# Attention and SwiGLU on one core: the next pair's q and k casts in three successive blocks, X loads behind the folds, four conversion steps earlier, one add on ScalarE

## The chip, the core and the metric

The kernel runs on one core of a Trainium2 chip. The metric is device time in microseconds from the start of the program to its end; three runs of the kernel before gave a median of 690.63 us (690.6 to 691.76). Engines are named as in the profile: PE is TensorE's matmul and PEld its weight load, DVE VectorE, ACT ScalarE, POOL GpSimd, and SP the engine that issues most DMAs from one queue.

## The reference

The program computes multi-head attention with rotary embeddings, and puts its output through a gated feed-forward layer. q, k and v are float32, the weights come in 64 bits, and the result is float32.

```
B, H, S, D = 4, 8, 576, 64          # attention
q, k  = rotate(q), rotate(k)
s     = (q @ k.T) / sqrt(D)
e     = exp(s - max(s))
attn  = e / (sum(e) + 1e-9) @ v
x     = attn as [2304, 512]
g     = x @ w_gate                  # [512, 1536]
y     = (g * sigmoid(g)) * (x @ w_val) @ w_out
```

## The kernel before, in words

**Two phases.** From about 11 to 277 us the kernel does attention; then, to 688 us, the feed-forward layer in products that TensorE runs almost without a gap. The 32 heads are taken as 16 pairs p. A pair has 9 blocks b of scores, and n = 9p + b numbers the blocks of the kernel. Loops run over n; in each block the named steps of PLAN["order"] (L31) are called, and tables in PLAN (L29 to L47) say in which block each step has something to do.

**One pair.** TensorE keeps float32 exact enough by splitting operands into a high and a low part. Scores of a block are four matmuls of 288 columns (L349), from QK, N and QZ, which hold the folded q and k; the ninth block takes six. ScalarE makes E with exp (L382), straight from the score's PSUM buffer sc, of which there are two. VectorE finds the maximum ahead of that (L364). TensorE transposes E through three PSUM buffers tr (L425; tails, the 64 columns left over, L435 and L437). ScalarE casts the transposed block to a high part (ET1h, ET2h, L426; TK1h, TK2h for tails, L440), and VectorE subtracts it for the low part (ET1l, ET2l, L427). The products with V (L465) use one PSUM buffer pv; ScalarE copies the result into Y (L470), and SP stores it (L484, L489, L490).

**The next pair.** Two pairs ahead, GpSimd rotates q and k into rot (L206 to L208) from X, which load_qk loads (L175). One pair ahead, the step qk_T has TensorE transpose the rotated q, k or their tail (L289, L293), and ScalarE and VectorE write high and low parts into N (cast L308, subtraction L312). After the third of these, qk_stack issues eight DMAs on SP, the folds (L319 to L326), that write QK, QZ and BD for the next pair's scores. PLAN["qk"] says in which block each of the three is done, and PLAN["qkw"] which one (2 is the tail, 0 is q, 1 is k). V is loaded as VR (L186) and split on GpSimd (L278, L279).

**Beside it.** During attention the first half of w_gate and w_val is converted from 64-bit to split float32: ten steps each (bits10), placed by PLAN["cv"], whose first entry is the block of the load (L772) and each further entry the block of one step. In pair 15 the second half begins, with its loads at L772 (f = 1) and steps on VectorE (L751 to L757). Attention's output comes back from memory as Xab (L637), is scaled by the reciprocal row sums R (L630) and split on GpSimd (L644 to L647). rsum (L389) adds 1e-9 to the row sums of four pairs and takes the reciprocal; rstore (L396) transposes and stores it.

**What sets the order.** GpSimd's instructions run in program order throughout attention, SP's until n = 48 (pair 5, block 3) and TensorE's until n = 9. All else in attention is put in an order by a scheduler, so that what the tables move also changes the order of instructions that no table names. `keep_in_program_order` takes one instruction out of that freedom. In the second phase all orders are written out by hand.

Of the kernel before, what the change touches and what calls it, by code (L numbers as in the profile page):

```python
# [14 lines left out]
ALU = mybir.AluOpType  # L15
# [13 lines left out]
    trb=3,  # L29
    warm=[9, 0, 1, 2, 0, 1],  # L30
    order=["qk", "scores", "trans", "pv", "exp", "evac", "rstore", "rope", "tails", "conv", "x", "conv1", "vsplit"],  # L31
    qk=[[3, 4, 6], [1, 2, 3], [0, 0, 1]],
    qkw=[[0, 2, 1], [2, 0, 1], [2, 0, 1]],
    tails=[4, 0],
    pv=[1, 6, 5, 3, 7, 8, 2, 7, 3],
    pv0=[0, 0, 0, 0, 0, 0, 10, 10, 2],
    lqk=0,
    lv=4,
    rope=1,
    vsplit=8,  # L40
    rstore=0,
    cv=[[13, 21, 25, 26, 28, 30, 34, 34, 44, 44, 45], [20, 30, 35, 36, 39, 41, 43, 43, 54, 54, 63]],
    xs=[[3, 3], [3, 6], [6, 5], [7, 5], [8, 7], [9, 5], [10, 5], [11, 5], [12, 7], [13, 7], [14, 1], [14, 2],
        [14, 8], [15, 0], [15, 2], [15, 4]],
    xe=[[5, 3], [6, 3], [7, 3], [8, 3], [9, 3], [10, 3], [11, 3], [12, 3], [13, 5], [14, 1], [14, 3], [14, 5],
# [68 lines left out]
class Attn:  # L114
# [274 lines left out]
    def rsum(self, b):  # L389
        nc = self.nc  # L390
        rt = self.rr_p.tile([128, 36], FP32, name="rt")
        nc.vector.tensor_scalar(out=rt, in0=self.sumt, scalar1=1e-9, scalar2=None, op0=ALU.add)
        nc.vector.reciprocal(out=rt, in_=rt)
        self.rt = rt

# [113 lines left out]
class Moe:  # L509
# [255 lines left out]
    def wfirst(self, f, i):  # L765
        if f == 0:
            tmp = self.again(f"xa1{'hl'[i]}", [128, 1536], U32, "raw")
        else:
            tmp = self.again(f"raw{i}", [128, (1536, 1024)[i]], U32, "raw")
        if (f, i) != (1, 1):  # L770
            self.X1 = tmp[:, 1024:1536]
        self.nc.sync.dma_start(out=tmp[:, 0:1024], in_=self.wsrc(i, f))  # L772
        raw, X = tmp[:, 0:1024].rearrange("p (f t) -> p f t", t=2), self.X1
        if f == 0:
            return self.bits10(raw, X, *self.Wb[f][i])
        return self.bits9(raw, X, *self.Wb[f][i], self.nc.gpsimd)
# [154 lines left out]
def attn_swiglu(ctx: ExitStack, tc: tile.TileContext, qk, vr, wg, wv, wo, main, tail, out):  # L931
    nc = tc.nc
# [5 lines left out]
    NP = B * H // 2  # L938
# [108 lines left out]
    P, cvq, cv1 = PLAN, {}, {}  # L1047
# [5 lines left out]
    for n in range(NB):  # L1053
        p, b = divmod(n, 9)
        if n == 9:
            ctl1.__exit__(None, None, None)
        if (p, b) == (NP - 1, 0):
            assert not any(cvq.values())
            early.close()
            moe.open_early(mctx, pl)  # L1060
        if n == 48:
            ctl0.__exit__(None, None, None)
        if n == 5:
            at.load_v(1)
        if b == (2 if 1 < p < 6 else P["lqk"]) and 0 < p < NP - 3:
            at.load_qk(p + 3)
        if b == (1 if p < 6 else P["lv"]) and 0 < p < NP - 1:
            at.load_v(p + 1)
        for name in P["order"]:
            steps[name](n, p, b)  # L1070
            if name == "qk" and n == P["qk"][0][2]:
                at.load_qk(3)
        if p == NP - 1 and ynext and NP - 2 in at.done:
            moe.yload(ynext.pop(0), 0)
# [432 lines left out]
```

## Time and profile before

| | |
|---|---|
| median of 3 runs | 690.63 us |
| the profiled execution | 690.11 us |
| its span, first to last instruction | 688.3 us |
| PE busy | 677.4 us (98%) |
| DVE busy | 582.4 us (85%) |
| ACT busy | 424.2 us (62%) |
| POOL busy | 470.1 us (68%) |

The shares are means over two phases. ScalarE is above 80% in most of attention and near 40% behind it, and GpSimd is nearly full in attention. PE's time is modelled from pipelined matmuls, so a busy PE does not tell where it waits; the waits of its weight loads (PEld) do.

### The profile page before, as it was taken

What the parts mean: (1) busy time and instruction counts of PE and PEld (TensorE: products, weight loads), DVE (VectorE), ACT (ScalarE), POOL (GpSimd) and SP (SyncE); (2) the same over time, 40 slices, a digit from 0 to 9 for tenths busy, and PEclk for the clock granted to TensorE, in tenths of its full rate; (3) what the DMA queues carried; (4) which work ended last, traced back from release to release, by engine and by line L of the source; (5) the groups of instructions that cost most, each with busy time, mean ns of one, the idle gap of its engine ahead of it and who ended that gap; (6) DMA issues with size and microseconds to landing.
All of it is one profiled execution on the core that took longest, in us unless ns stands there. A gap on an engine that the chain in (4) does not pass through costs nothing. (4 is left out here: it accounts for less than half of the span.)

```text
span 688.3 us, 12675 instructions
## 1 busy us (share of the span) xinstructions
PE 677.4 (98%) x4414; PEld 664.3 (97%) x4414; DVE 582.4 (85%) x883; ACT 424.2 (62%) x873; POOL 470.1 (68%) x475
## 2 busy tenths in 40 slices
PE   7999999999999999999999999999999999999998
PEld 6899999999999999999999999999999999999997
DVE  5888898888888888979988898988999599877683
ACT  5899988888888888555543434424435375344341
POOL 8899799999999985998889588677784720000000
PEclk9999999999999999999999999999999999999999
DMA  6897999889988879791214345354464797627101
GB/s 195 185 248 205 218 225 243 208 206 243 246 206 208 220 189 285 187 235 70 90 58 164 122 141 204 130 187 150 161 212 163 264 317 252 207 74 247 47 24 69
DMA packets 78784, 125.76 MB, mean 183 GB/s; under 512 B 16880, under 2 KB 55680, under 8 KB 78720
## 3 DMA queue, kind: packets, MB, share of 16 engines
q1 hardware_dynamic: 75248, 118.77, 60.6%
q10 hardware_dynamic: 3472, 6.18, 2.4%
q8 instruction: 35, 0.57, 0.4%
q14 instruction: 29, 0.24, 0.1%
HBM read 66.91 MB, written 33.10 MB: 145 GB/s over the span
## 5 line engine op out<-in xcount | busy, mean ns | idle before, releaser
L364 DVE TENSOR_REDUCE nmt<-sc 128x1 f32<-128x576 f32 x144 | 108.2, 751 | 20.3 <-PE sc L349 18.9
L382 ACT ACTIVATE E<-sc,nmt 128x576 f32<-128x576 f32 x128 | 97.5, 761 | 1.7 <-DVE nmt L364 1.6
L425 PE MATMUL tr<-ident,E 128*128 128x128 f32 x512 | 77.1, 274 | 0.4 <-DVE ET1l L427 0.2
L425 PEld LDWEIGHTS tr<-ident,E 128*128 128x128 f32 x512 | 61.2, 141 | 3.4 <-PE tr L289 1.3
L1472 PE MATMUL ch<-dW,dO 128*128 128x384 f32 x216 | 63.8, 337 | 0.2 <-DVE dW L1420 0.2
L206 POOL TENSOR_TENSOR t<-X,tab 128x256 f32<-128x256 f32 (+2 forms) x94 | 54.4, 600 | 9.4 <-DMA X<-in_qk_dram 5.8
L349 PE MATMUL sc<-QK 128*128 128x288 f32 x240 | 58.7, 325 | 1.4 <-ACT E L382 0.6
L426 ACT CAST ET2h<-tr 128x512 fp32r<-128x512 f32 x80 | 47.2, 590 | 14.0 <-PE tr L425 13.7
L427 DVE TENSOR_TENSOR ET2l<-tr,ET2h 128x512 fp32r<-128x512 f32 x80 | 53.1, 682 | 2.1 <-ACT ET2h L426 2.0
L349 PE MATMUL sc<-N,QZ 128*128 128x288 f32 x240 | 51.3, 296 | 0.0
L695 POOL TENSOR_TENSOR W<-WF,W 128x1024 fp32r<-128x1024 f32 x20 | 48.1, 2409 | 3.8 <-ACT W L695 3.7
L208 POOL TENSOR_TENSOR rot<-rot,t 128x512 f32<-128x512 f32 (+2 forms) x47 | 47.0, 999 | 3.7
L427 DVE TENSOR_TENSOR ET1l<-tr,ET1h 128x512 fp32r<-128x512 f32 x64 | 43.0, 685 | 7.0 <-ACT ET1h L426 6.7
L207 POOL TENSOR_TENSOR rot<-X,tab 128x512 f32<-128x512 f32 (+2 forms) x47 | 47.0, 1001 | 0.0
L1472 PE MATMUL ch<-dH,dO 128*128 128x384 f32 x156 | 45.5, 337 | 0.0
L426 ACT CAST ET1h<-tr 128x512 fp32r<-128x512 f32 x64 | 36.9, 597 | 13.1 <-PE tr L425 13.1
L842 PE MATMUL ch<-T2h,W 128*128 128x384 f32 x160 | 44.2, 337 | 0.0
L842 PE MATMUL ch<-T0h,W 128*128 128x384 f32 x160 | 44.2, 337 | 0.0
L842 PE MATMUL ch<-T1h,W 128*128 128x384 f32 x160 | 44.1, 336 | 0.0
L465 PE MATMUL pv<-ET2h,VS 128*128 128x320 f32 x128 | 40.8, 329 | 1.1 <-ACT ET2h L426 0.9
L349 PEld LDWEIGHTS sc<-QK 128*128 128x128 f32 x240 | 36.9, 190 | 4.3 <-ACT E L382 4.1
L1472 PEld LDWEIGHTS ch<-dW,dO 128*128 128x128 f32 x216 | 39.8, 188 | 0.5 <-DVE dW L1420 0.5
(349 smaller groups left out, 2300.7 us busy)
## 6 DMA issues: line engine op xcount, KB each, us to landing
QK<-N SPq DMA_DIRECT2D x64, 288.0 KB, 4.3
hd<-sg SPq DMA_DIRECT2D x14, 768.0 KB, 3.3
dB<-hd SPq DMA_DIRECT2D x8, 1152.0 KB, 7.3
X<-in_qk_dram SPq DMA_DIRECT2D x15, 576.0 KB, 5.6
yd<-Y SPq DMA_DIRECT2D x31, 256.0 KB, 5.7
raw<-in_moe_w_gate_dram SPq DMA_DIRECT2D x12, 512.0 KB, 3.7
raw<-in_moe_w_val_dram SPq DMA_DIRECT2D x12, 512.0 KB, 4.0
Xab<-yd SPq DMA_DIRECT2D x32, 192.0 KB, 4.9
```

The source lines that it names most:

```text
L206: e.tensor_tensor(out=sel(t2, u), in0=sel(x, w), in1=tb(Sn, u), op=ALU.mult)
L207: e.tensor_tensor(out=o, in0=x, in1=tb(C, slice(0, D)), op=ALU.mult)
L208: e.tensor_tensor(out=o, in0=o, in1=t2, op=ALU.add)
L349: nc.tensor.matmul(ps[:, g, 0:288], l, rr[:, o + g * 288:o + (g + 1) * 288], start=(x == 0), stop=(x == len(terms) - 1))
L364: nc.vector.tensor_reduce(out=nmcol, in_=ps[:, :, 0:288], axis=AX.XY, op=ALU.max, negate=True)
L382: nc.scalar.activation(out=E.rearrange("p (a b) -> p a b", a=2), in_=ps[:, :, 0:288], func=ACTF.Exp, bias=nmcol, scale=1.0, accum_out=self ...
L425: nc.tensor.transpose(ps[:, c], E[:, o + c * 128:o + (c + 1) * 128], self.ident)
L426: nc.scalar.copy(dst[0], src)
L427: nc.vector.tensor_tensor(out=dst[1], in0=src, in1=r32(dst[0]), op=ALU.subtract)
L695: return [lambda: self.nc.scalar.copy(h, f), lambda: le.tensor_tensor(out=l, in0=f, in1=r32(h), op=ALU.subtract)]
L842: nc.tensor.matmul(acc, l[:, w, c * 128:(c + 1) * 128], r, start=(n == 0 and k not in ONTO), stop=(n == 5), skip_group_check=True)
L1472: nc.tensor.matmul(ps, l, r[:, f], start=(new and f == 0 and x == 0), stop=(f == NFP - 1 and x == 2), skip_group_check=True)
```

## The change

The change has five parts. (1) From pair 2 on, tail, q and k of the next pair are transposed and cast in blocks 0, 1 and 2 instead of 0, 0 and 1; the folds follow the third. (2) The load of X for pair p + 3 is called in block 3 of each pair from 2 on (before: block 2 for pairs 2 to 5, block 0 behind that). (3) Four conversion steps of the first weight half move: w_gate's high copy on ScalarE and its mask on VectorE from block 34 to 30 and 31, w_val's scaling on ScalarE from 35 to 33 and its clamp on GpSimd from 36 to 34. (4) The add of 1e-9 goes from VectorE to ScalarE. (5) The loads of the second weight half keep their program order on SP.

```diff
--- before.py
+++ after.py
@@ -29,17 +29,16 @@
     trb=3,
     warm=[9, 0, 1, 2, 0, 1],
     order=["qk", "scores", "trans", "pv", "exp", "evac", "rstore", "rope", "tails", "conv", "x", "conv1", "vsplit"],
-    qk=[[3, 4, 6], [1, 2, 3], [0, 0, 1]],
+    qk=[[3, 4, 6], [1, 2, 3], [0, 1, 2]],
     qkw=[[0, 2, 1], [2, 0, 1], [2, 0, 1]],
     tails=[4, 0],
     pv=[1, 6, 5, 3, 7, 8, 2, 7, 3],
     pv0=[0, 0, 0, 0, 0, 0, 10, 10, 2],
-    lqk=0,
     lv=4,
     rope=1,
     vsplit=8,
     rstore=0,
-    cv=[[13, 21, 25, 26, 28, 30, 34, 34, 44, 44, 45], [20, 30, 35, 36, 39, 41, 43, 43, 54, 54, 63]],
+    cv=[[13, 21, 25, 26, 28, 30, 30, 31, 44, 44, 45], [20, 30, 33, 34, 39, 41, 43, 43, 54, 54, 63]],
     xs=[[3, 3], [3, 6], [6, 5], [7, 5], [8, 7], [9, 5], [10, 5], [11, 5], [12, 7], [13, 7], [14, 1], [14, 2],
         [14, 8], [15, 0], [15, 2], [15, 4]],
     xe=[[5, 3], [6, 3], [7, 3], [8, 3], [9, 3], [10, 3], [11, 3], [12, 3], [13, 5], [14, 1], [14, 3], [14, 5],
@@ -389,7 +388,7 @@
     def rsum(self, b):
         nc = self.nc
         rt = self.rr_p.tile([128, 36], FP32, name="rt")
-        nc.vector.tensor_scalar(out=rt, in0=self.sumt, scalar1=1e-9, scalar2=None, op0=ALU.add)
+        nc.scalar.add(rt, self.sumt, 1e-9)
         nc.vector.reciprocal(out=rt, in_=rt)
         self.rt = rt
 
@@ -769,7 +768,9 @@
             tmp = self.again(f"raw{i}", [128, (1536, 1024)[i]], U32, "raw")
         if (f, i) != (1, 1):
             self.X1 = tmp[:, 1024:1536]
-        self.nc.sync.dma_start(out=tmp[:, 0:1024], in_=self.wsrc(i, f))
+        ld = self.nc.sync.dma_start(out=tmp[:, 0:1024], in_=self.wsrc(i, f))
+        if f:
+            self.tc.keep_in_program_order(ld)
         raw, X = tmp[:, 0:1024].rearrange("p (f t) -> p f t", t=2), self.X1
         if f == 0:
             return self.bits10(raw, X, *self.Wb[f][i])
@@ -1062,7 +1063,7 @@
             ctl0.__exit__(None, None, None)
         if n == 5:
             at.load_v(1)
-        if b == (2 if 1 < p < 6 else P["lqk"]) and 0 < p < NP - 3:
+        if b == (3 if p > 1 else 0) and 0 < p < NP - 3:
             at.load_qk(p + 3)
         if b == (1 if p < 6 else P["lv"]) and 0 < p < NP - 1:
             at.load_v(p + 1)
```

The scheduler's order on TensorE at the first blocks of pair 7 was this (sc is a score buffer, tr a transpose buffer, rot the rotated q and k, Et the ninth block of the pair before):

```order
L349 MATMUL sc_2050<-QK1_112 128x288 x2
L349 MATMUL sc_2050<-N1_111,QZ1_114 128x288 x2
L289 MATMUL tr_2043<-ident_146,rot_1855 128x128 x4
L425 MATMUL tr_2056<-ident_146,Et_2011 128x128 x4
L349 MATMUL sc_2087<-QK1_112 128x288 x2
L349 MATMUL sc_2087<-N1_111,QZ1_114 128x288 x2
L435 MATMUL tr_2064<-ident_146,E_1907 128x128
L435 MATMUL tr_2064<-ident_146,E_1966 128x128
L437 MATMUL tr_2064<-ident_146,Et_2011 128x2x64
L349 MATMUL sc_2125<-QK1_112 128x288 x2
```

And now (line numbers are one lower):

```order
L348 MATMUL sc_2041<-QK1_112 128x288 x2
L348 MATMUL sc_2041<-N1_111,QZ1_114 128x288 x2
L424 MATMUL tr_2047<-ident_146,Et_2011 128x128 x4
L348 MATMUL sc_2070<-QK1_112 128x288 x2
L348 MATMUL sc_2070<-N1_111,QZ1_114 128x288 x2
L434 MATMUL tr_2055<-ident_146,E_1907 128x128
L434 MATMUL tr_2055<-ident_146,E_1966 128x128
L436 MATMUL tr_2055<-ident_146,Et_2011 128x2x64
L464 MATMUL pv_2083<-ET2h_142,VS0_115 128x320
L288 MATMUL tr_2063<-ident_146,rot_1838 128x128 x4
L348 MATMUL sc_2123<-QK1_112 128x288 x2
```

The four transposes of q moved from ahead of Et's to just ahead of the third scores, and one product with V comes between.

On ScalarE at the start of pair 4 (N is the cast of the next pair's q, raw a weight under conversion, FO the high part of a converted one) the order was this:

```order
L727 CAST FO_84<-raw_663 128x512
L382 ACTIVATE E_1261,sumt_1248<-sc_1243,nmt_1249 128x576
L470 COPY Y0_1167<-pv_1227 128x256
L724 ACTIVATE raw_862<-raw_862 128x512
L308 CAST N1_111<-tr_1273 128x512
L426 CAST ET2h_142<-tr_1286 128x4x2x64
L382 ACTIVATE E_1261,sumt_1248<-sc_1280,nmt_1249 128x576
```

And now:

```order
L469 COPY Y0_1168<-pv_1230 128x256
L425 CAST ET2h_142<-tr_1253 128x4x128
L384 COPY Et_1238<-Et_1238 128x64
L391 ACTIVATE rt_1241<-sumt_239 128x36
L307 CAST N1_111<-tr_1269 128x3x64
L381 ACTIVATE E_1263,sumt_1250<-sc_1245,nmt_1251 128x576
L425 CAST ET2h_142<-tr_1280 128x4x2x64
L381 ACTIVATE E_1263,sumt_1250<-sc_1274,nmt_1251 128x576
```

Between the two exps there is only the cast ET2h left; FO, raw and the Y copy stand earlier, N later, and the add of rsum (L391) ahead of the first exp.

On SP around the loads of the second weight half, in pair 14 and 15 (yd is the memory that takes Y):

```order
L637 DMA Xab<-yd_57 64x2x384 x2
L772 DMA raw<-in_moe_w_gate_dram 128x1024
L772 DMA raw<-in_moe_w_val_dram 128x1024
L780 DMA raw<-in_moe_w_gate_dram 128x1024 x2
L637 DMA Xab<-yd_57 64x2x384
L484 DMA yd_57<-Y_3992 128x2x256
```

And now:

```order
L636 DMA Xab<-yd_57 64x2x384 x2
L781 DMA raw<-in_moe_w_gate_dram 128x1024
L629 DMA R<-rd 64x4x384 x2
L483 DMA yd_57<-Y_3992 128x2x256
L636 DMA Xab<-yd_57 64x2x384 x2
L771 DMA raw<-in_moe_w_gate_dram 128x1024
L771 DMA raw<-in_moe_w_val_dram 128x1024
```

The two loads of L772 stood ahead of the store of Y_3992 and stand behind it and two Xab loads now; the L780 loads of w_gate moved ahead of them. From the end of attention on, the order of every engine is the same as before.

## Rows read from the trace of the kernel before

**Rows 1.** Stretches: length, busy us by engine (instructions), clock, DMA share, GB/s

```profile
129.34:145.80 16.46, 16.36 (x131) 15.95 (x130) 14.39 (x24) 14.57 (x39) 15.73 (x19) 1.00 0.82 203
...
300.00:500.00 200.00, 200.00 (x1141) 198.85 (x1141) 174.38 (x295) 93.48 (x149) 160.94 (x129) 1.00 0.41 140
```

**Rows 2.** TensorE's weight-load waits, 112.88 to 261: line, releaser: total us, times, longest

```profile
PEld sc L349 <- ACT E L382: 2.8, 9, 0.3
PEld tr L425 <- PE tr L289: 1.2, 7, 0.2
PEld pv L465 <- ACT ET2h L426: 0.8, 2, 0.4
```

**Rows 3.** The same waits, 45 to 98, pairs 2 to 5

```profile
PEld pv L465 <- ACT ET2h L426: 1.2, 1, 1.2
PEld sc L349 <- ACT E L382: 1.1, 2, 0.6
PEld tr L435 <- PE pv L465: 0.3, 1, 0.3
PEld tr L425 <- DVE ET2l L427: 0.3, 1, 0.3
...
```

**Rows 4.** Timeline of weight loads, pairs 3, 4, 7: start, length, operation, [idle before]

```profile
64.50 0.30 PEld L349 LDWEIGHTS sc<-QK 128*128 128x128 f32 x2 [0.62 <-ACT E L382]
...
81.58 0.19 PEld L465 LDWEIGHTS pv<-ET2h,VS 128*128 128x128 f32 x1 [1.18 <-ACT ET2h L426]
...
132.02 0.30 PEld L349 LDWEIGHTS sc<-QK 128*128 128x128 f32 x2 [0.34 <-ACT E L382]
133.34 0.42 PEld L425 LDWEIGHTS tr<-ident,E 128*128 128x128 f32 x4 [0.17 <-PE tr L289]
```

**Rows 5.** Timeline of ScalarE at the start of pairs 4 and 7

```profile
79.86 0.71 ACT L724 ACTIVATE raw<-raw 128x512 f32<-128x512 uint32 x1
80.43 0.61 ACT L308 CAST N<-tr 128x512 fp32r<-128x512 f32 x1
80.89 0.64 ACT L426 CAST ET2h<-tr 128x512 fp32r<-128x512 f32 x1
...
130.65 0.59 ACT L308 CAST N<-tr 128x512 fp32r<-128x512 f32 x1 [0.19 <-PE tr L289]
131.13 0.75 ACT L382 ACTIVATE E<-sc,nmt 128x576 f32<-128x576 f32 x1
```

**Rows 6.** Timeline of GpSimd: the first rope instruction of pair 4, pair 7's split

```profile
80.12 0.60 POOL L206 TENSOR_TENSOR t<-X,tab 128x64 f32<-128x64 f32 x2 [3.76 <-DMA X<-in_qk_dram]
...
129.53 1.58 POOL L279 TENSOR_TENSOR VS<-VR,VS 128x640 fp32r<-128x640 f32 x1
```

**Rows 7.** Timeline of SP: the first and last of pair 7's four QK folds

```profile
135.75 0.61 SPq L319 DMA_DIRECT2D QK<-N  x1
...
138.05 1.50 SPq L323 DMA_DIRECT2D QK<-N  x1
```

**Rows 8.** The last QK fold (L323), all pairs

```profile
DMA to landing us min/median/max: 3.9/4.6/7.1
```

**Rows 9.** Timeline of TensorE: the first scores of pair 8

```profile
143.49 0.51 PE L349 MATMUL sc<-QK 128*128 128x288 f32 x2
```

**Rows 10.** Timelines, pairs 14 and 15: a Y copy; SP's Xab and raw loads

```profile
261.91 0.38 ACT L470 COPY Y<-pv 128x256 f32<-128x256 f32 x1
...
259.54 1.26 SPq L637 DMA_DIRECT2D Xab<-yd  x2
260.90 0.57 SPq L772 DMA_DIRECT2D raw<-in_moe_w_gate_dram  x1
```

**Rows 11.** The raw loads of L772, issue to landing

```profile
DMA to landing us min/median/max: 6.8/7.1/7.5
```

**Rows 12.** Timeline of VectorE in pair 15: the first step of the second weight half

```profile
269.07 0.71 DVE L751 TENSOR_SCALAR raw<-raw 128x512 uint32<-128x512 uint32 x1
```

**Rows 13.** The add of rsum on VectorE: ns min/median/max, first and last start

```profile
L392 DVE TENSOR_SCALAR rt<-sumt x4: 173/261/693, 78.1 to 279.5; 128x36 f32<-128x36 f32 x4
```

## The prediction

> **What bounds the kernel now.** I began with the busy time by stretch [rows 1]. In the second phase TensorE is busy through all of 300 to 500 us, in attention for 16.36 us of the 16.46 of a pair; the granted clock is 1.00 (2.4 GHz) in both, so the clock is no term of the sum. A busy matmul engine is modelled, so next I read what its weight loads waited for, by line: in pairs 6 to 15 they waited 4.8 us in three rows [rows 2], in pairs 2 to 5 3.5 us in seven rows, of which the four largest stand [rows 3]. These 8.3 us are what an edit of the attention order can win at most; the rest is TensorE's own work, which the change leaves alone. Then I looked at where the waits sit [rows 4]: once a pair, at its blocks 0 to 2, and they name ScalarE (an exp, or the cast ET2h). ScalarE is not full, but at that spot its queue is [rows 5]: behind the exp stand the pair's last Y copy, a cast of the next pair's q or k and, in pair 4, a conversion step of a weight.
>
> **The moved conversion steps.** In pair 4 the scaling of raw starts at 79.86 and the cast N at 80.43; they push ET2h to 80.89, and TensorE waits 1.18 us for it and 0.34 more for the matmul behind [rows 3 to 5]. The change takes the scaling out of this place (0.57 from its start to the next) and the cast N (0.46): 1.03 us in all. TensorE then comes to the tails, which need ET2h's buffer, so a rest is left. I take **+1.0**, bounds 0.5 and 1.52 (both waits).
>
> The same steps return elsewhere on ScalarE, one to three blocks earlier. There TensorE is not waiting for it, so I price them at nothing; if that cover is gone, each costs its 0.57 once. On GpSimd the clamp of w_val goes ahead of the split of V. That costs GpSimd nothing while it waits 3.76 us for X anyway [rows 6], and delays the split by the clamp's time if the split was wanted; it is not, by the slack below.
>
> **The casts over blocks 0, 1 and 2.** Of the 3.5 us in pairs 2 to 5 the 1.52 of pair 4 are spoken for; 2.0 are left for pairs 2, 3 and 5, in pieces of which the largest is pair 3's 0.62, for an exp behind a Y copy and a cast N [rows 3, 4]. The order behind the change has one cast where two stood, but ScalarE still does both within three blocks. I take four tenths, **+0.8**, bounds 0 and 2.0.
>
> A steady pair is pair 7. TensorE waits 0.34 for the exp that starts at 131.13 and 0.17 for a transpose buffer [rows 4, 5]. By the new order q's four transposes move from ahead of Et's transposes to just ahead of the third scores, and one product with V comes between. So Et's transposes end 0.43 us earlier, ET2h goes ahead of the exp on ScalarE instead of the cast N, and the exp starts when it did, since ET2h waits for TensorE there where the cast waited before. What TensorE gains at the third scores is one product with V more to do before it must wait: 0.15 of the 0.34. The wait for the buffer (0.17) goes too, since q's transposes no longer stand right ahead of E's. Against that, k's cast now lies one block later, among exps that TensorE needs soon: it occupies ScalarE for 0.48 (from the cast at 130.65 to the exp at 131.13 in rows 5), which costs between nothing and all of it; I take 0.15, nearer to nothing because ScalarE is idle 1.9 us of a pair [rows 1]. The sum is 0.32 less 0.15, about 0.16 a pair, and for the nine pairs from 6 to 14 **+1.4**. The bounds are the whole 4.8 of rows 2, and, with the 0.48 fully paid, 0.16 lost in each pair, 1.4 in all.
>
> **The X loads behind the folds.** They were one or two blocks earlier in the program. X is wanted by the rope on GpSimd. Rope in pair 4 already waits 3.76 us for its X [rows 6], and the folds, ahead of X in SP's queue, now start about a block later, so the Xs of pairs 2 to 4 come 1 to 3 us later and the ropes of pairs 3 to 5 with them. GpSimd is busy 15.73 of 16.46 us [rows 1]: it wins back 0.7 us a pair. What hides this is the slack of the split of V: it ended at 131.11 [rows 6], and by the new order only the four QK folds stand behind its VR load. From the first of these to the last is 2.30 us on SP [rows 7] and the last lands 4.6 after its issue [rows 8], with the VR load some 7.3 after the split, 138.4. The first scores that need them start at 143.49 [rows 9]: 5.1 us of slack, 3.1 once TensorE runs 2 us earlier. A delay of 1 to 3 us fits. I take **0**; the price with the cover gone is the first rival.
>
> **The raw loads of the second weight half in pair 15.** They keep the program's place on SP, behind a store of Y that they stood ahead of. That Y is copied at 261.91 and done at 262.3 [rows 10]; the store and two loads of Xab that SP issues next (1.26) put the raw load at about 264.2 instead of 260.90. With a landing time of 6.8 [rows 11] it is there at 271.0, and VectorE reads it at 269.07, with reductions and casts queued behind [rows 12]. So VectorE waits up to 1.9 us. The two loads of w_gate that competed with it now go ahead, so it should land sooner; I take 1.0. VectorE is full from there until the split into FO, so the wait travels to TensorE but for what the exps have in hand. The add that leaves VectorE (below) gives some back. I take **-0.4** for the two, bounds +0.3 and -1.9.
>
> **The add of 1e-9 on ScalarE.** Four instructions on 128x36. On VectorE they took 0.17 to 0.69 [rows 13], 1.4 us over the kernel (both ends and twice the median), all beside TensorE's work but the last, which stands in pair 15's full stretch and is counted there. ScalarE then does them behind the exp of block 8 and a copy, where TensorE has the PV products to do. No row shows this add on ScalarE; its bounds are nothing and the 0.69 of VectorE's worst. I take 0.3 each, hidden. The rows show the same instruction in 0.17 and in 0.69. The Trainium skill, page "SBUF — State Buffer", section "Who interferes with whom", says that a tensor_scalar of VectorE in a two-port mode and GpSimd exclude each other, the later one blocked for the whole instruction; the spread agrees with that, and no run here shows its cause. The page "ScalarE: Activation LUTs", section "Rules for kernel authors", speaks against the edit: an add belongs on VectorE; with it the add would cost no more where it is now, and the sum would stay within the 0.3 taken.
>
> **The sum.** +1.0 +0.8 +1.4 +0 -0.4 = 2.8 us. The profiled execution took 690.11 (span 688.3 and 1.8 around it), so it would take 687.3. The median of the runs is 690.63, 0.5 above; from there the forecast is **687.8**.
>
> **Rival 1: GpSimd becomes the bound, slower.** If the Xs land later than 3 us (the folds wait for the casts, X behind them), ropes and the split of V come late, VR waits on SP ahead of QK, and the first scores of a pair wait with nothing else for TensorE. From a delay of 3.1 us on TensorE stalls by what exceeds it; at 5.9 the 2.8 are gone, and at 8 us it is 4.9 of stall, 692.7. For it: GpSimd has 0.7 us a pair to spare. Against: the estimate is 1 to 3 us, and X was already behind the folds in these pairs' queue. Chance 0.12.
>
> **Rival 2: handed back, the same.** The change doesn't do what it says at the steady crossings: ScalarE has the same work in the same three blocks, the third scores wait for the same exp, and pair 15's raw load costs the whole 1.9. Then 1.8 from the early pairs less 1.9 is about nothing: 690.6; with half of the raw wait 689.7. For it: the wait in rows 4 names an exp whose start does not move. Chance 0.20.
>
> **Rival 3: all crossings clear.** The 4.8 of rows 2 go and the early pairs give their 1.8: 684.0. It needs exps that start earlier, and ET2h's wait for TensorE speaks against that. Chance 0.08.
>
> **How the numbers follow.** The forecast has 0.60 and rival 3 0.08, both faster by over 0.2% (1.4 us, about what a measurement of this kernel can tell from no change): 0.68. Rival 2 gives within 0.2%: 0.20. Rival 1 gives slower: 0.12. The range: below, 684.4 takes in the early pairs at their bounds (+1.7) with half of what rows 2 leave beyond the 1.4; above, the steady term at its bound of -1.4 alone brings the sum to 690.6, and half of what pair 15 can still cost to 691.2. Rivals 1 and 3 lie outside with 0.20.
>
> **What would show it.** Right: TensorE's weight loads wait in pair 4 for ET2h under 0.4 us; in pairs 6 to 14 the wait for the exp is about 0.2 and that for the transpose buffer gone; rope starts in pairs 4 to 6 no more than 3 us later; a wait of VectorE for raw at pair 15 of about 1 us; attention ends 2 to 3 us earlier, and the phase behind it takes as long as before. Wrong: first scores of a pair that wait for a DMA (rival 1), a wait at raw of 2 us or more (rival 2), or a cast of k that TensorE waits for in every pair.

## The result, and the profile after

The changed kernel takes **699.99 us**, median of four executions (698.19 to 703.73), against 690.82 for the kernel before beside it (690.60 to 691.76): a ratio of 1.0137, 95% interval 1.0090 to 1.0184. The forecast was 687.8, at most 691.2; slower was given 0.12. The profiled execution took 703.73, its span is 701.9, 13.6 longer than before; it is the slowest of the four, 3.7 above their median, so the parts below add up to more than the median loss of 9.2. In its rows line numbers are one lower than before up to the raw loads (L771), and one higher behind them.

Where the 13.6 arose is read from the first exp of each pair (ScalarE's timeline, L381 and L382), in us:

```
pair                       2      3      4      5      6      7      8      9
before                 16.56  16.78  17.70  16.29  16.46  16.46  16.64  16.46
after                  16.62  17.53  17.26  16.80  16.20  16.34  16.45  17.73

pair                   10+11     12     13     14     15 (to its last exp)   behind it
before                 32.92  16.65  16.46  16.25  15.64                     411.5
after                  33.55  16.45  16.22  17.60  25.32                     412.1
```

Pairs 2 to 5 lost 0.9 in sum, 6 to 8 won 0.6, 9 to 14 lost 2.8, pair 15 alone lost 9.7, and the second phase 0.6; pairs 0 and 1 ended 0.2 later. Each trace is one execution: the changed kernel, e1 and e5 (two of the experiments below) have the same order on every engine up to pair 14, and took 17.73, 17.02 and 17.31 in pair 9 and 17.20, 16.44 and 16.45 in pair 10, so a part of what pairs 9 to 11 lost here is scatter. So the change did what it was to do at pair 4 and at the steady pairs 6 to 8, and lost most of its time at the end of attention.

First what TensorE's weight loads waited for in pairs 2 to 5 (columns: engine, line, releaser: total us, times, longest). It is 3.1 us where it was 3.5 [rows 3]: the wait for ET2h is gone, and waits for exps have taken its place.

```profile
PEld sc L348 <- ACT E L381: 1.9, 2, 1.0
PEld tr L424 <- PE sc L348: 0.5, 1, 0.5
PEld sc L348 <- ACT Et L381: 0.5, 1, 0.5
PEld tr L434 <- DVE ET2l L426: 0.2, 1, 0.2
```

The same view for 246 to 300 us, pairs 14 and 15. Before, these waits were 0.3, 0.2 and 0.2; now one of them is 6.9:

```profile
PEld sc L348 <- ACT E L381: 7.1, 2, 6.9
PEld sc L348 <- ACT Et L381: 1.6, 1, 1.6
PEld pv L464 <- DVE ET2l L426: 0.2, 1, 0.2
```

The wait names an exp, but ScalarE was not its cause. The maximum that an exp needs (L363) stands in VectorE's queue behind a conversion step, and that step waited. VectorE's timeline of pair 15 (start, length, operation, [idle before, released by]):

```profile
279.86 0.95 DVE L750 TENSOR_SCALAR raw<-raw 128x512 uint32<-128x512 uint32 x1 [7.18 <-DMA raw<-in_moe_w_gate_dram]
280.73 0.74 DVE L363 TENSOR_REDUCE nmt<-sc 128x1 f32<-128x576 f32 x1
```

And TensorE's weight loads, where that wait arrives:

```profile
282.39 0.50 PEld L348 LDWEIGHTS sc<-QK 128*128 128x128 f32 x2 [6.85 <-ACT E L381]
```

So VectorE stood 7.18 us at the first step of the second weight half, where the prediction had put 1.0 and, as its limit, 1.9. The reason is in SP's queue (start, length of the issue, DMA). Of the kernel after:

```profile
253.16 0.62 SPq L636 DMA_DIRECT2D Xab<-yd  x1
253.88 1.95 SPq L318 DMA_DIRECT2D QK<-N  x1
...
257.67 1.23 SPq L322 DMA_DIRECT2D QK<-N  x1
258.94 1.26 SPq L636 DMA_DIRECT2D Xab<-yd  x1
...
267.23 1.24 SPq L629 DMA_DIRECT2D R<-rd  x2
268.56 0.56 SPq L483 DMA_DIRECT2D yd<-Y  x1
269.21 1.61 SPq L636 DMA_DIRECT2D Xab<-yd  x2
270.87 0.77 SPq L771 DMA_DIRECT2D raw<-in_moe_w_gate_dram  x1
```

And before, the same stretch:

```profile
248.96 1.26 SPq L637 DMA_DIRECT2D Xab<-yd  x2
250.32 0.61 SPq L319 DMA_DIRECT2D QK<-N  x1
...
252.63 1.34 SPq L323 DMA_DIRECT2D QK<-N  x1
254.07 2.87 SPq L637 DMA_DIRECT2D Xab<-yd  x2
257.04 1.23 SPq L630 DMA_DIRECT2D R<-rd  x2
```

Before, both halves of a load of Xab stood ahead of the four QK folds. Now the folds start 3.6 us later (2.0 of it because pair 14 itself starts later), and one half stands behind them; it is issued at 258.94 instead of 249.6, and GpSimd starts on it 6.2 us after that, before 3.6 (253.19 below): of the 11.9 us that it comes later, 9.3 are the issue and 2.6 the landing. Next, R stands on SP at 267.23 instead of 257.04: SP's waits name GpSimd.

```profile
SPq L629 <- POOL xa1h L691: 3.7, 1, 3.7
```

GpSimd's timeline before and after shows the ring. Each Xab is scaled twice, the second time by R (L644), and split (L691, L646). The load of R goes into a buffer that this second scaling reads; its row in SP's waits is labelled with the instruction just behind. Before:

```profile
253.19 1.02 POOL L644 TENSOR_TENSOR Xab<-Xab 128x384 f32<-128x384 f32 x1 [2.35 <-DMA Xab<-yd]
...
264.11 1.02 POOL L645 TENSOR_TENSOR Xab<-Xab,R 128x384 f32<-128x384 f32 x1 [1.67 <-DMA R<-rd]
```

After:

```profile
265.10 1.01 POOL L643 TENSOR_TENSOR Xab<-Xab 128x384 f32<-128x384 f32 x1 [10.38 <-DMA Xab<-yd]
266.19 1.02 POOL L644 TENSOR_TENSOR Xab<-Xab,R 128x384 f32<-128x384 f32 x1
267.29 0.51 POOL L691 TENSOR_SCALAR xa1h<-Xab 128x384 fp32r<-128x384 f32 x1
...
274.82 1.02 POOL L644 TENSOR_TENSOR Xab<-Xab,R 128x384 f32<-128x384 f32 x1 [2.59 <-DMA R<-rd]
```

The chain, with its times: folds a block later; half an Xab behind them; GpSimd idle 10.38 us for it; the scaling by R ends at 267.21, and R's issue, which waited 3.7 us, starts at 267.23; a store of Y and two loads of Xab behind R; only then the raw load (270.87, before 260.90 [rows 10]); it lands as VectorE starts at 279.86, 9.0 after its issue (before 6.8 [rows 11]).

### The profile page after: what moved, and what is told of

It is laid out like the page before. It is cut to its first block, busy times and chain, and to the rows that moved or that the text cites. A ratio compares the mean times of both kernels' runs of the same rounds, so it can differ in the third digit from the quotient of the medians.

```text
span 701.9 us, 12756 instructions
## 1 busy us (share of the span) xinstructions
PE 680.6 (97%) x4414; PEld 667.6 (95%) x4414; DVE 584.3 (83%) x879; ACT 427.4 (61%) x877; POOL 470.1 (67%) x475
## 5 line engine op out<-in xcount | busy, mean ns | idle before, releaser
L363 DVE TENSOR_REDUCE nmt<-sc 128x1 f32<-128x576 f32 x144 | 108.3, 752 | 24.9 <-PE sc L348 24.6
L381 ACT ACTIVATE E<-sc,nmt 128x576 f32<-128x576 f32 x128 | 97.3, 760 | 15.1 <-DVE nmt L363 15.0
L348 PE MATMUL sc<-QK 128*128 128x288 f32 x240 | 59.7, 330 | 11.9 <-ACT E L381 8.2
```

Of the source, the lines that this page charges most:

```text
L348: nc.tensor.matmul(ps[:, g, 0:288], l, rr[:, o + g * 288:o + (g + 1) * 288], start=(x == 0), stop=(x == len(terms) - 1))
L363: nc.vector.tensor_reduce(out=nmcol, in_=ps[:, :, 0:288], axis=AX.XY, op=ALU.max, negate=True)
L381: nc.scalar.activation(out=E.rearrange("p (a b) -> p a b", a=2), in_=ps[:, :, 0:288], func=ACTF.Exp, bias=nmcol, scale=1.0, accum_out=self ...
```

## The experiments

Four quantities are read from each profiled execution: the longest wait of GpSimd for Xab in pairs 14 and 15; when attention's last exp (Et of pair 15) starts; how long after it the last xb1l, the last input of the second phase from GpSimd, is done; and the time from that exp to the end of the span. All in us, with the median time and its ratio to the kernel before on the same chip:

```
                       Xab wait  last exp  xb1l behind it  rest of span  median  ratio [95%]
before                     2.35*   276.82             8.7         411.5  690.8   
after                     10.38    289.81             9.9         412.1  699.99  1.0137 [1.0090, 1.0184]
e1_no_pin                 10.12    279.13            15.8         418.4  699.45  1.0119 [1.0104, 1.0134]
e2_casts_alone             9.56+   278.64             9.1         411.4  694.73  1.0057 [1.0039, 1.0076]
e3_conversion_alone       11.56    277.88            15.0         416.7  696.55  1.0074 [1.0056, 1.0091]
e4_no_casts                2.67    279.18             8.0         411.1  691.82  1.0007 [0.9997, 1.0017]
e5_xab_ahead               5.83    281.71             8.7         410.9  693.52  1.0042 [1.0027, 1.0056]
e6_xab_ahead_old_x         5.14    278.78             8.3         411.7  692.08  1.0020 [1.0008, 1.0032]
e7_xab_ahead_old_x_no_pin  5.06    279.98             9.2         411.5  692.62  1.0025 [1.0010, 1.0039]
e8_pair14_old              8.98    283.54             6.7         410.2  696.79  1.0075 [1.0058, 1.0093]
e9_best_guess              9.80    279.26            13.0         415.2  696.98  1.0087 [1.0066, 1.0108]
e10_add_alone              2.32*   278.31             8.8         412.2  691.22  1.0000 [0.9989, 1.0010]
e11_before_xab_late       12.97    278.15            15.8         418.4  697.51  1.0094 [1.0078, 1.0109]
e12_gains_only             3.35*   278.86             8.7         411.1  691.73  1.0013 [1.0002, 1.0025]
* the wait at this load; a later one (3.73, 4.71 and 4.13) costs nothing, since the last xb1l is not late
+ at the next load, which stands behind the folds and R on SP; pair 14's load of block 2 has both halves ahead of them and waited 1.02
```

The table holds the main finding already. It is not the wait itself that costs: in the traced execution of e2 GpSimd waited 9.56 us, xb1l was no later than in others, and the second phase took 411.4. Where xb1l is done within about 10 us of the last exp, the second phase takes 410.2 to 412.2; at 13.0 it takes 415.2, at 15.0 416.7, at 15.8 418.4. Where the lateness is met ahead of the last exp instead (after, e8), that exp is late; e5's is late in part because the first scores of pair 15 waited 2.27 us.

### The first set: which part

**e1_no_pin.** The first theory (A) was that the kept program order of the raw loads, called the pin from here on, is the cause.

```diff
-        if f:
-            self.tc.keep_in_program_order(ld)
```

> The changed kernel without its fifth part: the loads of the second weight half are left to the scheduler. TensorE, VectorE, ScalarE and GpSimd have the same order as in the changed kernel; only SP differs. Theory A (the pinned raw loads make pair 15 long, 25.3 us against 15.6): pair 15 falls to 16 to 17 us, the wait of VectorE for raw (7.18 us) goes, and the time is 690 to 692. Rival (the pin is innocent, POOL's late R and Xab loads keep pair 15 long): pair 15 stays over 22 us and the time over 697. The waits at the first scores of pairs 10 and 15 (1.7 and 1.6 us) should stay in either, if they come from folds that land late (theory B).

It measured 699.45, so A fell. The raw load left early (252.27), pair 15 was back near 16 us, and no wait for raw was left on VectorE. But GpSimd waited as before (10.12), and the same time was lost behind attention. TensorE's waits, 285 to 330:

```profile
PEld pv L465 <- ACT Y L470: 2.3, 1, 2.3
PEld ch L794 <- ACT sv L808: 1.8, 1, 1.8
```

Neither row stands in this stretch before. The first follows from the late GpSimd: the copy of Y stands on ScalarE behind a step of the second phase that waited for xb1l.

```profile
288.37 0.49 ACT L808 ACTIVATE Xab<-ch 128x384 f32<-128x384 f32 x1 [2.57 <-POOL xb1l L647]
288.75 0.42 ACT L470 COPY Y<-pv 128x320 f32<-128x320 f32 x1
```

The second names ScalarE again, further on; its own cause was not followed. The waits at the first scores of pairs 10 and 15 stayed, as 1.00 and 0.95 us. So the pin decides where the late GpSimd is paid, not whether.

**e2_casts_alone**: the kernel before with the table `qk` alone.

```diff
-    qk=[[3, 4, 6], [1, 2, 3], [0, 0, 1]],
+    qk=[[3, 4, 6], [1, 2, 3], [0, 1, 2]],
```

> The kernel before with the casts over blocks 0, 1 and 2 and nothing else of the change. Theory B (the folds, a block later, land too late where other loads stand among them on SP): some pairs' first scores wait, 2 to 4 us in all, the other pairs win about 0.15 each, time 690.5 to 693. Rival (the casts are the gain that the prediction took them for): no pair waits at its first scores, 688 to 689.

It measured 694.73, above both ranges, but its profiled execution was the lowest of four (691.76), so the trace doesn't show where the others lost 2.5 to 4.1 us more. Pairs 6 to 13 took 16.20 to 16.45: 0.2 to 0.3 less than before, more than the forecast 0.16. Of first scores, pair 15's alone waited, 1.43. Pair 4, with the old conversion steps in the same blocks as the new casts, took 19.42 (before 17.70), and pair 14 17.43. GpSimd waited 9.56 for the next Xab, not for the one of pair 14's block 2 (1.02).

**e3_conversion_alone**: the table `cv` alone.

```diff
-    cv=[[13, 21, 25, 26, 28, 30, 34, 34, 44, 44, 45], [20, 30, 35, 36, 39, 41, 43, 43, 54, 54, 63]],
+    cv=[[13, 21, 25, 26, 28, 30, 30, 31, 44, 44, 45], [20, 30, 33, 34, 39, 41, 43, 43, 54, 54, 63]],
```

> The kernel before with the four conversion steps moved and nothing else. The prediction's own term: pair 4 loses its 1.18 us wait for ET2h and about 1 us in length, time 689.4 to 690. Rival (the scheduler's new order on SP, where a raw load stands among pair 14's folds, costs as much as pair 4 gives): 690.3 to 692.

Pair 4 went from 17.70 to 16.90: the term of 1.0 is worth **0.8** by itself. But the kernel took 696.55. Four numbers for pairs 3 to 5 had shifted the scheduler's choices as far as pair 14: one half of the Xab load is ahead of the folds, the other among three behind them, and GpSimd waited 11.56. The loss sits in the second phase, in the rows of e1 and two more. This run was not expected to lose, and it took the suspicion off the casts themselves.

**e4_no_casts**: the changed kernel with the old `qk` table.

> The changed kernel with the old blocks for the casts (0, 0, 1). The pinned raw loads stand ahead of pair 14's Y store there, not behind it. Theory B: no pair waits at its first scores. Theory A in its milder form: the raw load is issued some 3 us earlier than in the changed kernel, so VectorE waits 2 to 4 us for it instead of 7.18, and the time is 690 to 693. Rival (the casts and not the pin make pair 15 late): VectorE does not wait for raw, 689 to 690.

691.82, ratio 1.0007 [0.9997, 1.0017]: the conversion steps, the X loads, the pin and the add together, and no loss that can be measured. On SP both halves of Xab are ahead of the folds, GpSimd waits 2.67, and VectorE 0.80 for raw. Together e3 and e4 point to the place of Xab among the folds, which a set of parts brings about, and not to one part of the change. e2 does not fit this: both halves are ahead of the folds, and the median is 3.4 us over the kernel before; what cost that stays open.

### The second set: the queue edge itself

**e5_xab_ahead.** The changed kernel, with the step "x" (the Xab load) called first in pair 14's block 2, ahead of the folds in the program. Of all engines only SP's order differs.

```diff
-        for name in P["order"]:
+        od = P["order"]
+        if (p, b) in ((14, 2),):
+            od = ["x"] + [o for o in od if o != "x"]
+        for name in od:
```

> The changed kernel whole, but in block 2 of pair 14 the Xab load is called before the casts instead of behind them. Only SP's order differs: both halves of that load stand ahead of pair 14's four QK folds, where the changed kernel has one half behind them, and the R load behind it and the pinned raw loads come sooner. Theory C (that half load is the root: GpSimd waits 10.4 us for it, R and the raw loads wait behind it on SP, and the second phase's inputs are late): GpSimd's longest wait for Xab in pairs 13 to 15 falls from 10.4 to under 4 us, VectorE's wait for raw from 7.2 to under 2, the last input half xb1l is done before 291 us instead of 299.7, time 691 to 693.5. Rival (the pin of the raw loads alone): nothing changes, over 697.

693.52: of the 9.2 us lost, 6.5 came back by a change of SP's order alone. SP's rows, and GpSimd's:

```profile
252.26 2.60 SPq L637 DMA_DIRECT2D Xab<-yd  x2
254.95 0.61 SPq L319 DMA_DIRECT2D QK<-N  x1
```

```profile
259.89 1.00 POOL L644 TENSOR_TENSOR Xab<-Xab 128x384 f32<-128x384 f32 x1 [5.83 <-DMA Xab<-yd]
```

GpSimd waited 5.83 (expected: under 4), VectorE at raw not at all. R and the raw loads stand further ahead on SP too (R at 263.13), so this run does not separate the half of Xab from the loads behind it. What remained sat in pairs 3, 5, 9, 14 and 15.

**e6_xab_ahead_old_x.** e5 with the old place of the X loads; again only SP differs.

```diff
-        if b == (3 if p > 1 else 0) and 0 < p < NP - 3:
+        if b == (2 if 1 < p < 6 else P["lqk"]) and 0 < p < NP - 3:
```

> The kernel of e5_xab_ahead with the X loads at their old blocks. TensorE, VectorE, ScalarE and GpSimd have the same order in both; only SP differs. If the X loads behind the folds cost what pairs 3, 9 and 10 lost in the changed kernel (0.8, 1.3 and 0.7 us): those are gone and the time is 2 to 3 us under e5, 688.5 to 690.5. Rival (the folds come a block later because of the casts, and that alone makes these pairs wait): the pairs keep their loss and the time is that of e5 within 1 us.

692.08. So the X loads behind the folds, which the prediction had priced at 0, cost about **1.4**, though the two intervals overlap from 1.0027 to 1.0032, and less than the 2 to 3 expected. In the profiles pairs 3, 4 and 5 took 17.02, 16.98 and 15.98 against 17.46, 17.36 and 16.79 in e5, 1.6 in sum; e7, with e6's order there, has the same three within 0.04. Pair 9 can't be counted: 16.72 in e6 is 17.22 in e7, in the same order. The first rope of pair 3 on GpSimd shows the difference. e5:

```profile
66.50 0.60 POOL L206 TENSOR_TENSOR t<-X,tab 128x64 f32<-128x64 f32 x2 [4.70 <-DMA X<-in_qk_dram]
```

e6:

```profile
61.68 0.59 POOL L206 TENSOR_TENSOR t<-X,tab 128x64 f32<-128x64 f32 x2
```

Before, this rope started at 61.48, and in the changed kernel at 66.27, 4.8 us later. In e4, with the X loads in their new place but the casts in the old blocks, it started at 63.82, and pairs 3 and 5 lost 0.1 and nothing, so in these pairs the delay that costs takes both parts (pair 6 did lose 0.65 there; its first scores waited 0.4 for QK). TensorE shows it in e5 as 0.4 us at the first scores of pair 4 and, in pair 5, 0.5 for the rotated q (rot); neither wait is there in e6.

**e7_xab_ahead_old_x_no_pin.** e6 without the pin (the diff of e1).

> The kernel of e6_xab_ahead_old_x without the pin of the raw loads; SP's order alone differs, the two raw loads of the second weight half trading places with a load of w_gate. Theory C: the pin matters only when the queue ahead of it is late, so the time is that of e6 within 1 us and VectorE waits for raw under 1 us in both. Rival (the pin costs by itself): 2 us or more under e6.

692.62 against 692.08, with spreads of 4 us: nothing can be told. Where Xab is on time the pin is worth nothing that is measured here.

### The third set: is the cause enough by itself, and can the gain be had?

**e10_add_alone**: the kernel before with the add of rsum on ScalarE.

```diff
-        nc.vector.tensor_scalar(out=rt, in0=self.sumt, scalar1=1e-9, scalar2=None, op0=ALU.add)
+        nc.scalar.add(rt, self.sumt, 1e-9)
```

> The kernel before with the add of 1e-9 on ScalarE and nothing else; SP's and GpSimd's order is that of the kernel before. The prediction's term: nothing that can be measured, 690 to 691. Rival (by the rule that an add belongs on VectorE, ScalarE at a pair's crossing has no room for it): a pair in four is longer by 0.3 us or more, and the time 691.5 or over.

691.22 against 691.27 of the kernel before beside it. The term was 0, and 0 it is. The Trainium skill, page "ScalarE: Activation LUTs", section "Rules for kernel authors", says to use VectorE for an add; four adds of 128x36 in the whole kernel are no case that shows a price for either engine.

**e8_pair14_old.** The changed kernel with the old blocks for the casts in pair 14 only, to bring Xab ahead of the folds.

```diff
+        if p in (14,):
+            bs = [0, 0, 1]
```

> The changed kernel whole, but in pair 14 alone the casts stand in the old blocks (0, 0, 1). Theory C, told from the other side: pair 14's folds are issued a block earlier again, the Xab load behind them with them, so GpSimd's long wait (10.4 us) falls under 4, pair 14 is back to 16.3 us and pair 15 to 16 to 17, and the time is 690.5 to 692, less than the 693.5 of e5_xab_ahead, since pair 15's first scores don't wait for folds either. Rival (it is the pinned raw loads, or the casts of all pairs): over 695.

The expectation missed. The folds went to 250.89, but Xab went behind them with both halves (254.90): the scheduler chooses SP's order anew from everything ahead. GpSimd waited 8.98, VectorE 5.24 at the first raw step, and the kernel took 696.79, which lies in the rival's range. It agrees with the cause, since Xab was late and the time too, but by its time alone it doesn't tell the cause from the rival; as a repair it failed.

**e9_best_guess.** The kernel before with the new conversion steps, and the new casts in all pairs from 2 but 9 and 14.

> A version made from what the runs showed: the conversion steps moved; the casts over blocks 0, 1 and 2, but in pairs 9 and 14, where R, Xab and raw loads stand among the folds, in the old blocks; X loads, the add and the raw loads as before. If attention's gains in pairs 4 to 8 and 10 to 13 (0.1 to 0.8 each) are kept and pairs 9, 14 and 15 are as before: 688 to 689.5, faster than both. Rival (the order that the scheduler then chooses on SP gives it back in the second phase's inputs): 690.5 to 693.

It measured 696.98. In the profile the first exp of pair 14 came 2.0 us earlier than before, so there is a gain up to there. Then Xab was behind the folds (252.97), GpSimd waited 9.80, pair 15 took 19.6, and the second phase 3.8 more than before.

**e11_before_xab_late.** The deciding run: nothing of the change at all. In the kernel before the Xab load of pair 14's block 2 is made to be issued behind the last QK fold.

```diff
-        d(out=QK[V, 1], in_=pair(N[V, 1, 0:576], 576))
+        self.tc.lastfold = d(out=QK[V, 1], in_=pair(N[V, 1, 0:576], 576))
...
-            pend.append((s, c, t, moe.xload(s, c, t)))
+            with tc.issue_after(tc.lastfold.ins) if (p, b) == (14, 2) else ExitStack():
+                pend.append((s, c, t, moe.xload(s, c, t)))
```

> The kernel before, none of the change in it, with one edge added: pair 14's Xab load is issued behind pair 14's QK folds on SP instead of ahead of them. TensorE, VectorE, ScalarE and GpSimd have the order of the kernel before; the scheduler rearranges SP around the edge (two raw loads and R move too). Theory C: GpSimd waits 8 to 11 us for that load instead of 2.4, the last input half xb1l is done at 291 to 295 us instead of 285.5, and the second phase waits for it: 694 to 698. Rival (the casts are needed for the loss; the queue's order alone is harmless): within 1 us of the kernel before.

697.51, ratio 1.0094 [1.0078, 1.0109]. All other engines have the order of before. SP, where the scheduler also moved the raw loads ahead of the folds and R behind (266.36; before 257.04):

```profile
252.71 1.17 SPq L323 DMA_DIRECT2D QK<-N  x1
253.97 4.26 SPq L637 DMA_DIRECT2D Xab<-yd  x4
```

GpSimd:

```profile
264.23 1.01 POOL L644 TENSOR_TENSOR Xab<-Xab 128x384 f32<-128x384 f32 x1 [12.97 <-DMA Xab<-yd]
```

TensorE's waits, 285 to 330, with the rows of e1 again:

```profile
PEld pv L465 <- ACT Y L470: 2.4, 1, 2.4
PEld ch L794 <- ACT sv L808: 2.1, 1, 2.1
PEld ch L794 <- DVE Xab L809: 1.2, 2, 0.6
PEld ch L794 <- ACT Xab L808: 0.3, 1, 0.3
```

And ScalarE's, of the same stretch:

```profile
ACT Xab L808 <- POOL xb1l L647: 2.5, 1, 2.5
```

TensorE's busy time over 276 to 330 us (length, busy us by engine, clock, DMA share, GB/s). e11:

```profile
276.00:330.00 54.00, 49.64 (x289) 47.79 (x289) 43.09 (x68) 27.23 (x54) 47.56 (x40) 1.00 0.68 169
```

Before:

```profile
276.00:330.00 54.00, 54.00 (x319) 53.80 (x318) 48.80 (x71) 29.95 (x57) 50.27 (x39) 1.00 0.62 154
```

SP's new order, with all four loads of Xab behind the four folds where two stood ahead, cost 6.6 us with every other engine's order untouched. What in that order costs is told apart only in part. R moved with Xab (it waits for GpSimd), as it does in the changed kernel. And the two raw loads ahead of the folds are a rival for the landing: GpSimd started on this Xab 11.0 us later than before, 6.0 of it by the issue of its second half (255.60 against 249.61) and 5.0 because it started 8.6 us after that issue, before 3.6. That Xab is late does not need them: e8 and e9 have no raw load there, their Xab behind the folds landed in 5.8 to 6.8 us, and GpSimd waited 8.98 and 9.80. How much of the 6.6 they add was not tested.

**e12_gains_only.** The kernel before with the new conversion steps, and the new casts in pairs 3, 4 and 5 alone, where [rows 3] had most to win; from pair 14 on, SP's order is that of before.

```diff
+        if p >= 2 and p not in (3, 4, 5):
+            bs = [0, 0, 1]
```

> A version from what the runs showed: the conversion steps moved, the casts over blocks 0, 1 and 2 in pairs 3, 4 and 5 only, nothing else of the change. On SP the order from pair 14 on is that of the kernel before, Xab ahead of the QK folds. Theory C: GpSimd's wait for Xab stays under 4 us, pairs 3 to 5 give 1 to 1.5 us, pairs 14 and 15 are as before: 689 to 690, faster than both kernels by 0.1 to 0.2%. Rival (loads elsewhere give it back): 690.5 to 692.

691.73, ratio 1.0013 [1.0002, 1.0025], so no gain. Xab was on time (3.35). Pair 4 won 0.6, pair 5 0.1, but pair 3 took 17.84 (before 16.78), pair 2 0.5 more and pair 15 1.0 more. Pair 2 has the order of before on every engine, so its 0.5 is scatter; and pair 15 took 16.55 in e10 and 16.33 in e11, so the 15.64 of before is a short one. No version here beat the kernel before.

## Why the prediction was wrong

**The step that failed** is the raw load of pair 15. The prediction let the store of Y and two loads of Xab stand ahead of it and came to an issue at 264.2. It did not ask when SP would be free to issue these: R stands ahead of them in the same queue, and R waits for GpSimd, which waited for Xab, which waited behind the folds that the change itself had moved. The issue was at 270.87, 6.7 later than put, and the landing took 9.0 instead of 6.8 (+2.2), where the prediction had it land sooner because the two loads of w_gate go ahead. To the 1.9 that the prediction had worked out before it took 1.0 these add 8.9; VectorE itself came 3.6 later (272.68, not 269.07), and 7.2 are left, which is the wait measured. The bound of 1.9 was worked out from the same queue and failed with it. The price of pair 15, forecast 0.4 and at most 1.9, was **9.7** in the traced execution; against the 16.55 of e10, which has SP's order of before, it is 8.8. That execution is the slowest of four, so in the median one the price is smaller by an amount that no trace shows.

The order of SP showed R and Xab around the raw loads, in the rows of the section on the change; what was missing was to follow the queue back from there to pair 14. The prediction had checked what the folds' new place does to the split of V, in a steady pair. Pair 14 is no steady pair: its queue carries, between the same folds, the inputs of the second phase.

**The cover behind attention** was the other half of it. The forecast took the second phase as it was. Its inputs come from GpSimd with a lead of which nothing was said, and the table shows how little is free beyond the 8.7 us of before: 9.9 cost at most 0.6, 13.0 cost 3.8.

**Pair 4's term** was right in kind and a little large. The wait for ET2h (1.18) left the list; by itself the edit won 0.8 (e3) of the forecast 1.0, and in the changed kernel 0.44, where a wait of 0.98 for an exp stands in the pair and, with the X loads at their old place (e6), 0.72. The 17.70 of before is 17.50 in e11 with the same order there, so these are good to some 0.2.

**The early pairs' +0.8** failed outright: pairs 2, 3 and 5 lost 0.06, 0.75 and 0.51. It was a share (four tenths) of waits whose cause had been read for one of them only. In the changed kernel the largest of their waits, 1.0, is for an exp again. The X loads are the larger part of it (next point): with them at their old place pairs 3 and 5 took 17.02 and 15.98 (e6). Why e12, without these, lost 1.1 in pair 3 stays open.

**The X loads at 0** were wrong: 1.4 (e5 against e6). The estimate had the Xs 1 to 3 us later; the rope of pair 3 came 4.8 later. That is rival 1's mechanism in kind, and by its scale (what exceeds 3.1) it would be 1.7. The sign named for it stayed silent: it asked for the ropes of pairs 4 to 6, and these came 1.5, 1.6 and 1.5 later; the late one was pair 3's. That the sizes agree is luck: the 3.1 was misread (under the steady pairs), and 0.5 of what e5 shows is q's transposes waiting for rot, where the rival had the first scores wait.

**The steady pairs' +0.16** held: pairs 6, 7, 8, 12 and 13 won 0.26, 0.12, 0.19, 0.20 and 0.24, and in e2 all of 6 to 13 won 0.2 to 0.3. In the changed kernel it was not nine of them, though. The first scores of pairs 10 and 15 waited for QK, 1.71 and 0.72 us in the one and 1.61 in the other, and pairs 9, 10 and 14 are longer by this; in e1, e5 and e8, with the same order up to there, pair 10's wait was 1.00, 1.29 and 0.56. TensorE's timeline at the end of pair 9 has the largest:

```profile
178.76 0.30 PEld L348 LDWEIGHTS sc<-QK 128*128 128x128 f32 x2 [1.71 <-ACT Et L381]
```

The row is labelled with Et, but the folds were late: pair 10's second wait ends at 181.9, just behind the landing of its last fold (181.80), and pair 15's at 262.6, just behind that of its second (262.50). The folds of that stretch, from issue to landing (of the four, two landings are on record):

```profile
DMA to landing us min/median/max: 6.7/7.5/8.3
```

Before, the last of a pair landed in 4.6 in the median [rows 8], and the folds of this pair started 1.3 us later (171.10 against 169.84 before), so most of the loss is some 3 us in the landing; R and Xab loads stand ahead of them on SP in this pair, before as well as after, and nothing showed what slowed the landing. The prediction's slack (5.1 us, 3.1 once TensorE runs earlier) was too large even for pair 7, where it was read: it let only the four QK folds stand behind the VR load. In the changed kernel's trace two BD and two QZ folds stand between them too, and the last QK fold is issued at 139.36, 6.8 us after the split of V ends (132.57), where the prediction had 2.7. The second and third QK folds landed at 142.13 and 143.53; the first scores of pair 8, at 144.23, did not wait.

**The add** was rightly at 0 (e10).

**The sign.** Rival 1 was the right family, GpSimd late through SP, at 0.12. It was put to X and the split of V, where the rows were, and priced at 4.9; the larger loss came by Xab, which it did not name. The gain itself was there at pair 14 in e9, 2.0 us, and was lost behind it.

## What to carry to other kernels

When an edit moves DMAs in a queue that issues in order, follow the queue at every place where it also carries something for another phase, not at a steady place alone, and ask of each load behind the moved one who waits for it and which load waits for him in turn. A gain at the full engine lasts only as far as the lead of the next phase's inputs: read that lead before the sum. And where a scheduler orders the queue, test a suspected edge by forcing it in the kernel before, since undoing a part of the change moves other edges too, and list what else the forced order moved: here two raw loads and R.

## What was not expected of the hardware

After TensorE's idle stretch in pair 15 its clock was low. Windows of the kernel after (as in [rows 1]: length, PE, PEld, DVE, ACT and POOL busy, clock, DMA share, GB/s):

```profile
276.00:282.40 6.40, 0.01 (x1) 0.01 (x1) 2.54 (x3) 0.89 (x3) 4.97 (x6) 0.89 1.05 246
282.40:288.00 5.60, 5.60 (x24) 5.27 (x25) 5.53 (x11) 3.35 (x9) 0.00 (x0) 0.52 1.10 252
288.00:300.00 12.00, 12.00 (x81) 11.92 (x80) 8.22 (x11) 6.45 (x15) 10.61 (x11) 1.00 0.15 43
```

TensorE did one matmul in 6.4 us; in the 5.6 us behind that the granted clock was 0.52, in effect the 1.2 GHz level, and from 288 on 1.00 again. So a wait of 6.85 us costs more than itself: by these rows up to 5.6 times 0.48, 2.7 us, if TensorE is the bound there. Pair 15's loss of 9.7 would be the wait of 6.85 and about that; that it is so is not shown, since VectorE was busy for 5.53 of the same 5.60. The low clock is seen in e1 too, where TensorE was busy for 2.0 of the 4 us from 286 to 290 (waiting for Y's copy):

```profile
290.00:292.00 2.00, 2.00 (x11) 2.00 (x10) 1.01 (x1) 0.43 (x1) 1.92 (x2) 0.65 0.05 13
292.00:294.00 2.00, 2.00 (x8) 2.00 (x7) 1.93 (x3) 0.00 (x0) 1.83 (x3) 0.50 0.39 131
294.00:300.00 6.00, 6.00 (x37) 6.00 (x36) 5.86 (x6) 2.55 (x5) 6.00 (x5) 1.00 0.76 195
```

The Trainium skill, page "TensorE: Matmul & The Clock Gate", section "What's actually happening", has the low level as the state that activity releases; the rows agree.

The landing time of the raw load rose from 6.8 to 9.0 us, though the DMA engines were full in both stretches (share 1.05 before, 1.04 after; 318 and 267 GB/s); why stays open. And executions of one kernel lay further apart than those of before: 698.2 to 703.7 for the changed kernel against 690.6 to 691.8. Why was not looked into.
